# FNet mixing plus gated MLP in split fp32: three instruction moves (y loads, column scaling, second token tile)

## The chip, the cores and the metric

One core of one Trainium2 chip runs the kernel. The metric is the device time of one execution in microseconds. A core has TensorE (PE, with PEld for its weight loads), VectorE (DVE), ScalarE (ACT), GpSimd (POOL) and SyncE (SP), each with an instruction stream of its own that runs in order; SP and POOL also issue DMA transfers, and a DMA issue that must wait holds up all that stands behind it in that stream.

## The reference

With x of 2048 tokens by 640 columns, the function is a sum of three terms over one layer norm:

```
xn  = layernorm(x)
a   = xn @ dft_hid_re.T ; b = xn @ dft_hid_im.T
A   = dft_seq_re @ a - dft_seq_im @ b
g   = xn @ W_gate ; h = (g * (g > 0)) * (xn @ W_up)
out = x + A + h @ W_down
```

All is fp32. W_gate and W_up are 640 x 1728, W_down is 1728 x 640, the sequence matrices are 2048 x 2048.

## The kernel before, in words

Every fp32 product is made of three fp32r matmuls: an operand is split into a high part (ACT copies it rounded, L124) and a low part (DVE subtracts, L125), and `mm3` (L126 to L132) issues high x high, high x low and low x high. On top of that the products use 2x2 block schemes with seven products in place of eight (the names B11, T1, B21, T2, B22, T3, T4).

There are three stages, one after the other on PE.

**Stage 1** (to about 399 us; the layer norm lies in its first 65 us): xn transposed times the sequence matrices. Tokens come in eight groups n = 0 to 7 of 256 tokens, each as two tiles j = 0, 1 of 128 tokens. Groups 0 to 3 lie in the SBUF tile `xs_early`, groups 4 to 7 in `xs_late`; NH = 4. Output columns come in chunks c. At the start the list of work alternates: chunk 0 with group n, then chunk 1 with group n. `first_stream` describes such an entry by a load, a preparation, a run and a finish; `drive(4, 2)` calls the load of an entry, its preparation two entries later, its run four later, its finish five later.

The layer norm of group n+1 is written into the preparation of entry (chunk 1, group n), by `next_group`. Its instructions are pinned: each engine runs them in the order in which they are written. For one group:

- DVE: batch statistics of both tiles (L204, L205), centring of tile 0 (`ln_center`, L225), a reciprocal (listed at L210), centring of tile 1 (L225), four small instructions of a refinement (L218 to L221), the low parts of tiles 0 and 1 (`ln_low`, L235). Groups 0 to 3 norm 384 of the 640 columns this way. The other 256 columns (slice K2, the "lower token columns") are scaled in place by two more instructions at L276, and `keep_a21` (L240) lets POOL issue a DMA that carries them to `xs_early`. Then comes the split of the sequence matrix for (chunk 1, that group), whose low part is L125.
- ACT: the square root (L210), the mean (L213), the high parts of tiles 0 and 1 (`ln_high`, L231), the high part of that split (L124), and the high part of the next chunk-0 matrix (L257).
- POOL: the DMA issue at L240, then one tiny instruction that waits for DVE's split (`behind_vector`, L248), then the two low parts of the next chunk-0 matrix (L255).

PE takes for each group 18 matmuls for chunk 0 (`next_products`, L481: first the six of tile 0 with the high parts of xn, then the six of tile 1, then six with the low parts) and 18 for chunk 1 (L130 to L132). The dictionary `late` carries handles: `late["high"]` and `late["ln"]` are the ACT and DVE instructions after which the chunk-1 split is to be issued.

Groups 0 to 3 of chunk 0 end in three PSUM banks. `keep_first`, called right after the run of group 3, copies them to SBUF on ACT (L121, into `sa`); group 4 then adds to the same banks, so its first three matmuls wait for the three copies.

**Stage 2** (about 399 to 735 us) forms gate and up in 26 rounds (`gate_up`) and a rest (`gate_up_rest`, L927, L928).

**Stage 3** (`project`, to the end) multiplies by the hidden matrices and W_down and adds x, for token half q = 1 and then q = 0. A product such as B11 runs over six units u = 0 to 5. Its entry loads an activation tile `rw` (L1069 from stage 1's results, L1071 from stage 2's) and a weight tile `wr` (L1100), splits both, and runs the matmuls. `get_y` (L1211) loads pieces of x transposed into tiles `y`; three of them belong to B11. It is an entry of its own in the list, placed behind unit 3. `add_y` (L1214) adds the result of a product to `y`. The order of SP and POOL in this stage is the order in which the list is written; DVE and ACT are ordered by the scheduler. The tiles `y` lie where operands of stage 2 lay.

Of the kernel before, what the change touches and what calls it, by code (L numbers as in the profile page):

```python
# [58 lines left out]
def fnet_reglu_kernel(  # L59
# [60 lines left out]
    def copy(o, i):  # L120
        return nc.scalar.activation(o, i, AF.Copy)  # L121
# [108 lines left out]
    def ln_high(g, xs, mv, j, cs):  # L230
        return nc.scalar.activation(ln_parts(g, j, cs)[0], xs[:, j, cs], AF.Copy, scale=mv[:, j, 4:5])  # L231
# [10 lines left out]
    def pin(steps):  # L242
        return [tc.keep_in_program_order(i) for i in steps]
# [6 lines left out]
    def next_group(g, b, raw, before):  # L250

        xs, bs, mv = ln_tiles(g)
        js = slice(0, SG)
        cs = K14 if g < NH else slice(0, D)
        low = lambda engine, j: pin([engine.tensor_tensor(flat(b, 1)[:, j], raw[:, j], flat(b, 0)[:, j].bitcast(F32), op=OP.subtract)])  # L255
        pin(ln_stats(g, xs, bs, mv, js))
        pin([nc.scalar.activation(flat(b, 0), raw, AF.Copy)])  # L257
        if before is not None:
            behind_vector(before)
            for j in range(SG):  # L260
                low(nc.gpsimd, slice(j * CH, (j + 1) * CH))
        root, inverse = ln_first(g, mv, js)
        pin([root])
        pin([ln_mean(g, mv, js)])
        pin([ln_center(xs, mv, 0, cs)])
        pin([inverse()])
        pin([ln_high(g, xs, mv, 0, cs)])
        pin([ln_center(xs, mv, 1, cs)])
        late["high"] = pin([ln_high(g, xs, mv, 1, cs)])[0].ins
        if before is None:  # L270
            for j in range(SG):
                low(nc.vector, slice(j * CH, (j + 1) * CH))
        pin(ln_refine(g, mv, js))
        late["ln"] = pin(ln_low(g, xs, j, cs) for j in range(SG))[-1].ins
        if g < NH:
            late["ln"] = pin(nc.vector.tensor_scalar(xs[:, j, K2], xs[:, j, K2], mv[:, j, 0:1], stat[:, 1, g, j : j + 1],  # L276
                                                     op0=OP.subtract, op1=OP.mult) for j in range(SG))[-1].ins
            keep_a21(g)
        if g == NG - 1:
            nc.sync.dma_start(rows.rearrange("m (g p j) -> p m g j", p=P, j=SG), stat)  # L280
        if g == 2:
            st = stage()[:, :CH].rearrange("p (j d) -> p j d", j=SG)
            for j in range(SG):
                late["high"] = pin([nc.scalar.activation(st[:, j], ln_place(0)[:, j, K2], AF.Copy, scale=stat[:, 1, 0, j : j + 1])])[0].ins
            keep_a21(0, st)

    def first_group(b):

# [244 lines left out]
    def first_stream(c, name, g):  # L533

        t = {}
        half = int(name == "B21")
        n = half * NH + g

        norm = {0: 0 if n == 0 else None, 1: n + 1 if n < NG - 1 else None}.get(c)

        def load():
            if n == 0 and c == 0:
                st = start["raw"] = [raw(), raw()]
                get = lambda c, j: nc.sync.dma_start(st[c][:, j * CH : (j + 1) * CH], dft[c, 0, 0][:, j * CH : (j + 1) * CH])
                ln_load(0, slice(0, 1))
                get(0, 0)
                get(1, 0)
                ln_load(0, slice(1, 2))
                get(0, 1)
                get(1, 1)  # L550
                return
            if norm is not None:
                tc.keep_in_program_order(ln_load(norm, slice(0, SG)))
            if n > 0 or c > 1:
                t["s"] = raw()
                nc.sync.dma_start(t["s"], dft[c, 0, n])
                start[c, n] = t

        def prepare():
            if norm == 0:  # L560
                start["b"] = [(parts(), st) for st in start["raw"]]
                first_group(start["b"])
                return
            if (n > 0 or c > 1) and "b" not in t:
                t["b"] = b = parts()
                with ExitStack() as order:
                    if c == 1:
                        order.enter_context(tc.issue_after(late["ln"]))
                        order.enter_context(tc.issue_after(late["high"]))
                    i = split(flat(b, 0), flat(b, 1), t["s"])  # L570
                if c == 1 and n < NG - 1:
                    late["ln"] = i.ins
            if norm is not None:
                t1 = start[0, norm]
                t1["b"] = parts()
                next_group(norm, t1["b"], t1["s"], flat(b, 1)[:, W2 - 1 : W2] if norm > 1 else None)

        def run():
            if n == 0 and c < 2:
                first_products(c, start["b"])  # L580
                return
            if n > 0 and c == 0:
                next_products(n, t["b"])
                if n == NH - 1:
                    keep_first()
                return
            accs = [(c, ("e1", i)) for i in range(2)]
            with ExitStack() as order:
                if n > 0 and c == 1:
                    order.enter_context(tc.issue_after(start["pe"]))  # L590
                product(g, t["b"], resident(n, 0), accs, half == 0, half == 1, ((c, "v1"), half, half == 0))

        def keep_first():
            t["first"] = sums_a()
            for i, key in enumerate((("e1", 0), ("e1", 1), "v1")):
                pin([copy(t["first"][:, i], E[c, key])])

        def finish():
            if g == NH - 1:
                s = t.get("first")  # L600
                if s is None:
                    s = (sums_a, sums_b)[c % 2]()
                    for i, key in enumerate((("e1", 0), ("e1", 1), "v1")):
                        copy(s[:, i], E[c, key])
                defer(1, lambda: nc.gpsimd.dma_start(pqd[c][0][:, :3] if half else firsts[c], s[:, :3]))

        todo.append((load, prepare, run, finish))
# [451 lines left out]
    def project(q):  # L1059
# [184 lines left out]
        for name in ("B11", "T1", "B21", "T2", "B22", "T3", "T4"):  # L1244
# [4 lines left out]
            for u in range(len(units)):  # L1249
                l, p, r = unit(name, u, u == 0)  # L1250
                end = u == len(units) - 1 and not (tiles and name != "T3")
                todo.append((l, p, r, (lambda name: lambda: read(name))(name) if end else idle))
                if u == 3:
                    todo.append(((lambda name: lambda: get_y(name))(name), idle, idle, idle))
                if name == "B21" and u in (0, 2):
                    (plain_rest if u else plain_block)()
# [50 lines left out]
```

## Time and profile before

| what | value |
|---|---|
| time, median of 3 | 1030.93 us (1029.65 to 1031.65) |
| the profiled execution | 1030.23 us, span 1028.3 us |
| PE busy | 1022.1 us, 4528 matmuls |
| PE weight loads busy | 844.5 us |
| DVE, ACT, POOL busy | 805.9, 427.6, 118.1 us |
| granted PE clock | 1.0 |
| DMA over the span | 236 GB/s |

The time of an execution and the span of its trace differ by 1.93 us, which lie outside the first and last recorded instruction. A timeline row gives the start in us, the length in us, the engine, the line, the operation with the tile written and the tile read, the count of merged instructions, and in brackets the idle time before it with what ended it. A matmul row shows 0.39 us, because matmuls overlap; the distance of two starts, about 0.227 us, is what one costs.

### The profile page before, as it was taken

Reading aid. Unit: us, or ns where it says so; the run is one execution under the profiler, and the core shown is the slowest. Engines: PE = TensorE matmul, PEld = TensorE weight load, DVE = VectorE, ACT = ScalarE, POOL = GpSimd, SP = SyncE. Lnnn points to the kernel's source line nnn. Section 1 sums busy time; section 2 is a strip of 40 time slices with the busy share of each in tenths; the row PEclk is TensorE's granted clock in tenths of the full one; section 3 lists DMA queues with packets and bytes.
Section 4 is the critical chain, followed back from the end, with each engine's and each line's share of the span. In section 5 each row is a group of like instructions: output and inputs, shape, how many; then the busy total and the mean of one; then the engine's idle time right before and its main releaser. Section 6 shows DMA issues by size and latency. Waiting matters only on the chain.

```text
span 1028.3 us, 12486 instructions
## 1 busy us (share of the span) xinstructions
PE 1022.1 (99%) x4528; PEld 844.5 (82%) x4528; DVE 805.9 (78%) x1089; ACT 427.6 (42%) x534; POOL 118.1 (11%) x184
## 2 busy tenths in 40 slices
PE   9999999999999999999999999999999999999998
PEld 7888888888888888888888888888888888888886
DVE  8967987998989586788878988886597666886764
ACT  5554453343433333433335443443355423552531
POOL 3431001012110002411110001000000000000000
PEclk9999999999999999999999999999999999999999
DMA  7987734968969785763474665662699647986543
GB/s 304 342 278 274 265 124 164 338 221 262 349 229 348 299 323 165 249 213 136 153 237 152 225 228 216 230 255 103 237 346 302 189 132 232 357 322 213 156 154 122
DMA packets 101469, 242.73 MB, mean 236 GB/s; under 512 B 11552, under 2 KB 50976, under 8 KB 98848
## 3 DMA queue, kind: packets, MB, share of 16 engines
q1 hardware_dynamic: 83664, 171.68, 48.6%
q0 software_dynamic: 17744, 70.26, 18.6%
q8 instruction: 35, 0.57, 0.2%
q14 instruction: 26, 0.21, 0.1%
HBM read 182.12 MB, written 58.74 MB: 234 GB/s over the span
## 4 chain that ended last, share of the span: by engine, by line
PE 98%; DMA 1%; DVE 0%; SPq 0%; ACT 0%; issue 0%; DVEq 0%
PE ps L132 31%; PE ps L131 31%; PE ps L130 31%; PE ps L481 3%; PE ps L1204 1%; PE ps L510 1%; DMA rw<-hd 1%; DMA r<-in_x 0%; SPq L1211 0%; DVE wt L125 0%; DVE bs L204 0%; DVE y L1214 0%; ACT cb L292 0%; SPq L1100 0%; SPq L1071 0%
## 5 line engine op out<-in xcount | busy, mean ns | idle before, releaser
L132 PE MATMUL ps<-cb,wt 128*128 128x512 f32 x390 | 151.9, 390 | 0.4 <-DVE wt L125 0.4
L130 PE MATMUL ps<-cb,wt 128*128 128x512 f32 x390 | 151.8, 389 | 0.0
L131 PE MATMUL ps<-cb,wt 128*128 128x512 f32 x390 | 151.7, 389 | 0.0
L125 DVE TENSOR_TENSOR cb<-rw,cb 128x1024 fp32r<-128x1024 f32 x83 | 94.0, 1132 | 68.4 <-ACT cb L124 66.9
L124 ACT ACTIVATE cb<-rw 128x1024 fp32r<-128x1024 f32 x83 | 82.0, 988 | 147.3 <-PE ps L132 127.6
L124 ACT ACTIVATE cb<-raw 128x1024 fp32r<-128x1024 f32 x71 | 75.3, 1060 | 114.2 <-PE ps L132 107.8
L125 DVE TENSOR_TENSOR cb<-raw,cb 128x1024 fp32r<-128x1024 f32 x71 | 86.8, 1222 | 40.3 <-ACT cb L124 40.1
L132 PE MATMUL ps<-xs_early,gw 128*128 128x512 f32 x260 | 101.2, 389 | 0.0
L131 PE MATMUL ps<-xs_early,gw 128*128 128x512 f32 x260 | 101.2, 389 | 0.0
L130 PE MATMUL ps<-xs_early,gw 128*128 128x512 f32 x260 | 101.1, 389 | 0.0
L130 PE MATMUL ps<-cb,xs_late 128*128 128x512 f32 x232 | 90.2, 389 | 0.0
L131 PE MATMUL ps<-cb,xs_late 128*128 128x512 f32 x232 | 90.2, 389 | 0.0
L132 PE MATMUL ps<-cb,xs_late 128*128 128x512 f32 x232 | 90.2, 389 | 0.0
L121 ACT ACTIVATE gw<-z 128x1024 fp32r<-128x1024 f32 (+1 forms) x52 | 57.6, 1109 | 76.4 <-DVE z L814 76.4
L131 PE MATMUL ps<-cb,xs_early 128*128 128x512 f32 x226 | 88.0, 390 | 0.0
L132 PE MATMUL ps<-cb,xs_early 128*128 128x512 f32 x226 | 87.9, 389 | 0.0
L130 PE MATMUL ps<-cb,xs_early 128*128 128x512 f32 x226 | 87.9, 389 | 0.0
L132 PEld LDWEIGHTS ps<-cb,wt 128*128 128x128 f32 x390 | 73.2, 188 | 16.0 <-DVE wt L125 0.7
L131 PEld LDWEIGHTS ps<-cb,wt 128*128 128x128 f32 x390 | 73.2, 188 | 15.4
L130 PEld LDWEIGHTS ps<-cb,wt 128*128 128x128 f32 x390 | 73.2, 188 | 15.2
L121 ACT ACTIVATE u<-ps 128x512 f32<-128x512 f32 x52 | 31.1, 597 | 94.0 <-PE ps L132 94.0
L824 DVE TENSOR_TENSOR gw<-z,gw 128x1024 fp32r<-128x1024 f32 (+1 forms) x52 | 64.6, 1283 | 3.8 <-ACT gw L121 3.8
(190 smaller groups left out, 1983.1 us busy)
## 6 DMA issues: line engine op xcount, KB each, us to landing
raw<-in_dft SPq DMA_DIRECT2D x94, 512.0 KB, 5.5
wt<-wparts SPq DMA_DIRECT2D x66, 256.0 KB, 3.2
z<-in_wgu SPq DMA_DIRECT2D x26, 640.0 KB, 4.0
hd<-ob POOLq DMA_DIRECT2D x26, 512.0 KB, 3.7
rw<-hd SPq DMA_DIRECT2D x24, 512.0 KB, 6.4
wparts<-pw POOLq DMA_DIRECT2D x11, 1024.0 KB, 4.1
tk<-in_dft SPq DMA_DIRECT2D x16, 512.0 KB, 6.1
set<-r POOLq DMA_DIRECT2D x16, 512.0 KB, 4.0
```

The source lines that it names most:

```text
L121: return nc.scalar.activation(o, i, AF.Copy)
L124: nc.scalar.activation(hi, src, AF.Copy)
L125: return nc.vector.tensor_tensor(lo, src, hi.bitcast(F32), op=OP.subtract)
L130: nc.tensor.matmul(ps, wh, mh, start=first, stop=False, skip_group_check=more)
L131: nc.tensor.matmul(ps, wh, ml, start=False, stop=False, skip_group_check=more)
L132: nc.tensor.matmul(ps, wl, mh, start=False, stop=last, skip_group_check=more)
L481: start["pe"] = pin([nc.tensor.matmul(E[0, key], xn_part(n * SG + j, d)[v == 1], b[:, int(v == 2), j], start=False, stop=n % NH == NH - 1 ...
L510: pin([nc.tensor.matmul(E[c, key], xn_part(j, d)[v == 1], b[c][0][:, int(v == 2), j], start=j == 0 and v == 0, stop=False)])
L824: tt(self.w[:, 1, cs], self.z[:, cs], self.w[:, 0, cs].bitcast(F32), op=OP.subtract)
L1204: nc.tensor.matmul(B[key], wr[:, v, es], hr[:, cs], start=False, stop=v == 1, skip_group_check=not new)
```

## The change

Three moves of instructions; the matmuls and their order on PE stay as they are, and so does the number of instructions of every kind.

1. `get_y` of B11 for q = 1 goes into the list behind unit 5 in place of unit 3.
2. The two scaling instructions of the lower token columns of groups 1, 2 and 3, with the DMA of `keep_a21`, move out of `next_group` into a function `scale_a21`, which is called right after the split of (chunk 1, that group).
3. For group 4 the high part of tile 1 on ACT and its low part on DVE are issued by `second`, which `keep_first` calls after the three copies.

```diff
@@ next_group
-        late["high"] = pin([ln_high(g, xs, mv, 1, cs)])[0].ins
+        if g != NH:
+            late["high"] = pin([ln_high(g, xs, mv, 1, cs)])[0].ins
...
-        late["ln"] = pin(ln_low(g, xs, j, cs) for j in range(SG))[-1].ins
+        late["ln"] = pin(ln_low(g, xs, j, cs) for j in range(SG)[: 1 if g == NH else SG])[-1].ins
+        if g == NH:
+
+            def second():
+                late["high"] = pin([ln_high(g, xs, mv, 1, cs)])[0].ins
+                late["ln"] = pin([ln_low(g, xs, 1, cs)])[0].ins
+
+            late["second"] = second
         if g < NH:
-            late["ln"] = pin(nc.vector.tensor_scalar(xs[:, j, K2], xs[:, j, K2], mv[:, j, 0:1], stat[:, 1, g, j : j + 1],
-                                                     op0=OP.subtract, op1=OP.mult) for j in range(SG))[-1].ins
-            keep_a21(g)
+            late["a21"] = g, xs, mv
...
+    def scale_a21():
+
+        if "a21" not in late:
+            return
+        g, xs, mv = late.pop("a21")
+        late["ln"] = pin(nc.vector.tensor_scalar(xs[:, j, K2], xs[:, j, K2], mv[:, j, 0:1], stat[:, 1, g, j : j + 1],
+                                                 op0=OP.subtract, op1=OP.mult) for j in range(SG))[-1].ins
+        keep_a21(g)
@@ first_stream, prepare
                 if c == 1 and n < NG - 1:
                     late["ln"] = i.ins
+                    scale_a21()
@@ first_stream, keep_first
                 pin([copy(t["first"][:, i], E[c, key])])
+            late["second"]()
@@ project
-                if u == 3:
+                if u == (len(units) - 1 if (name, q) == ("B11", 1) else 3):
                     todo.append(((lambda name: lambda: get_y(name))(name), idle, idle, idle))
```

## The prediction

> **What bounds the kernel now.** I read the head of the page first, then PE's timeline for every place where two matmul starts lie farther apart than usual, then the waits of PEld, and last the rows of the other engines around those places.
>
> ```profile
> span 1028.3 us, 12486 instructions
> PE 1022.1 (99%) x4528; PEld 844.5 (82%) x4528; DVE 805.9 (78%) x1089; ACT 427.6 (42%) x534; POOL 118.1 (11%) x184
> ```
>
> PE is busy for 99% of the span, and the change leaves it every matmul. So the change can only touch the few holes in PE's stream, or dig new ones. After the start, a matmul begins 0.227 us after the one before it (between the L481 rows at 23.05 and 31.21 lie 36 matmuls, so 8.16/36). These are the places that matter here:
>
> ```profile
> 18.71 0.39 PE L130 MATMUL ps<-cb,xs_early 128*128 128x512 f32 x1
> 19.06 0.50 PE L131 MATMUL ps<-cb,xs_early 128*128 128x512 f32 x1
> 19.40 0.40 PE L132 MATMUL ps<-cb,xs_early 128*128 128x512 f32 x1
> ...
> 23.05 4.24 PE L481 MATMUL ps<-cb,xs_early 128*128 128x512 f32 x18
> ...
> 31.21 4.24 PE L481 MATMUL ps<-cb,xs_early 128*128 128x512 f32 x18
> ...
> 39.37 4.52 PE L481 MATMUL ps<-cb,xs_late 128*128 128x512 f32 x18
> ```
>
> ```profile
> 745.34 0.39 PE L131 MATMUL ps<-cb,wt 128*128 128x512 f32 x1
> 746.08 0.50 PE L132 MATMUL ps<-cb,wt 128*128 128x512 f32 x1 [0.35 <-DVE wt L125]
> 746.42 0.40 PE L130 MATMUL ps<-cb,wt 128*128 128x512 f32 x1
> ```
>
> ```profile
> PEld ps L481 <- ACT sa L121: 0.5, 2, 0.3
> PEld ps L131 <- DVE cb L125: 0.4, 1, 0.4
> ```
>
> Hole 1, at 18.71: distances 0.35 and 0.34 in place of 0.227, so 0.24 us; PEld names DVE's split of chunk 1, group 1. Hole 2, at 39.37: eighteen matmuls of group 4 take 4.52 where those of group 3 take 4.24, so 0.28 us; PEld names the copies into `sa`. Hole 3, at 745.34: distances 0.74 and 0.34, so 0.51 + 0.11 = 0.63 us; PE waited for a weight split of B11's unit 4. After each hole the next matmul is late by about 0.11 too, so I count every stall as its wait plus 0.11. The three holes are 1.15 us together: **no more than that can be won**, 0.11% of the time.
>
> **Move 1, the y loads.** The queue of SP, the consumer of the load, and the first use of `y`:
>
> ```profile
> 726.28 0.48 SPq L1100 DMA_DIRECT2D wr<-in_wd  x1
> 735.10 1.29 SPq L1211 DMA_DIRECT2D y<-in_xt  x3
> 736.44 0.43 SPq L1071 DMA_DIRECT2D rw<-hd  x1
> 736.91 0.47 SPq L1100 DMA_DIRECT2D wr<-in_wd  x1
> ...
> 738.57 1.51 SPq L1069 DMA_DIRECT2D rw<-pq  x1
> ```
>
> ```profile
> SPq L1211 <- PE ps L132: 4.0, 1, 4.0
> ```
>
> ```profile
> 742.84 1.06 ACT L124 ACTIVATE cb<-rw 128x1024 fp32r<-128x1024 f32 x1 [7.16 <-DMA rw<-hd]
> ```
>
> ```profile
> 733.50 0.95 DVE L125 TENSOR_TENSOR wt<-wr,wt 128x768 fp32r<-128x768 f32 x1
> ...
> 755.60 0.68 DVE L1214 TENSOR_TENSOR y<-ps,y 128x512 f32<-128x512 f32 x1
> ```
>
> SP issues nothing from 726.76 to 735.10, because the first y load waits for the last matmul of stage 2, whose memory it takes. Behind it stand the loads of units 4 and 5. ACT gets unit 4's activations at 742.84, that is 6.4 us after their issue at 736.44. With y behind unit 5, the loads of unit 4 and the activations of unit 5 can be issued from 726.8 on. Their tiles are free: `raws` has 24 buffers, and unit 4's weights are the fourth tile of four. Unit 5's weights must wait for the first tile of four to be read, by the DVE row that ends at 734.45. Counting 6.4 to 7.5 us from about 727, unit 4 is there by 734.5, and its split comes right behind unit 3's, some 6 us earlier. Hole 3 goes: **minus 0.63 us**. The y loads themselves still start at 735.1, since the release is PE's, and land some 5 to 7 us later, long before 755.60. What is late next: the loads of T1, issued from 738.57, now follow y directly at about 736.4, so they too are earlier by 2 us. I find no new wait there.
>
> **Move 2, the scaling.** The rows of group 1's tail and group 2's norm on DVE, then POOL:
>
> ```profile
> 17.14 0.73 DVE L276 TENSOR_SCALAR r<-r,mv,stat 128x256 f32<-128x256 f32 x2
> 17.79 1.22 DVE L125 TENSOR_TENSOR cb<-raw,cb 128x1024 fp32r<-128x1024 f32 x1
> 18.93 0.88 DVE L204 BATCH_NORM_STATS2 bs<-r 128x6 f32<-128x320 f32 x2
> ...
> 20.96 1.06 DVE L225 TENSOR_SCALAR r<-r,mv 128x384 f32<-128x384 f32 x1
> ...
> 22.01 0.40 DVE L225 TENSOR_SCALAR r<-r,mv 128x384 f32<-128x384 f32 x1
> ...
> 23.20 1.15 DVE L235 SCALAR_TENSOR_TENSOR xs_early<-r,stat,xs_early 128x384 fp32r<-128x384 f32 x2
> 24.26 0.94 DVE L276 TENSOR_SCALAR r<-r,mv,stat 128x256 f32<-128x256 f32 x2
> ```
>
> ```profile
> 18.20 0.88 POOL L240 DMA_DIRECT2D xs_early<-r  x1 [4.72 <-DVE r L276]
> 19.11 0.20 POOL L248 TENSOR_TENSOR root_t<-cb 128x1 f32<-128x1 f32 x1
> 19.25 2.54 POOL L255 TENSOR_TENSOR cb<-raw,cb 128x512 fp32r<-128x512 f32 x2
> ```
>
> The split moves from 17.79 to 17.14, which fills hole 1: **minus 0.24 us**. Split plus scaling take as long as before, so the statistics still start at 18.93. But the instruction order of the changed kernel keeps POOL's L240 ahead of L248 and L255. Today the DMA issue (0.88, starting 0.33 after the scaling's end) runs beside the split and costs POOL nothing. Behind the change the scaling ends at about 19.0, the issue runs from 19.35 to 20.2, and POOL's two low parts start at 20.4 in place of 19.25: **1.1 us later, for each of groups 1 to 3**. PE does not need those parts for 2 us more. DVE does feel them: the first L225 row takes 1.06 against 0.40 for the second; it starts at 20.96 and ends at 22.02, 0.2 after POOL's pair has ended at 21.79. So centring cannot run while POOL subtracts. What happens when it is due in the first of two subtractions, a later place shows:
>
> ```profile
> 42.88 2.86 POOL L255 TENSOR_TENSOR cb<-raw,cb 128x512 fp32r<-128x512 f32 x2 [0.40 <-ACT cb L257]
> ```
>
> ```profile
> 44.09 0.50 DVE L225 TENSOR_SCALAR r<-r,mv 128x640 f32<-128x640 f32 x1
> ...
> 44.63 1.47 DVE L225 TENSOR_SCALAR r<-r,mv 128x640 f32<-128x640 f32 x1
> ```
>
> The first centring slips in between POOL's two halves (they take 2.86 in place of 2.54), and only the second waits to the end. With POOL 1.1 later, every group from 2 to 4 comes into this case. The Trainium skill, SBUF — State Buffer, section "SBUF: two separate sides", says that the shared ports of VectorE and GpSimd are an exclusive lock, held for one whole instruction; the rows just shown agree, 0.50 for the centring that got in and 1.47 for the one that did not. If the lock were handed on only after POOL's pair, the sum would be that of rival B.
>
> ACT's rows for group 2 give what follows a centring:
>
> ```profile
> 22.13 1.12 ACT L231 ACTIVATE xs_early<-r,mv 128x384 fp32r<-128x384 f32 x2 [0.66 <-DVE mv L210]
> 23.16 0.89 ACT L284 ACTIVATE st<-r,stat 128x256 f32<-128x256 f32 x2
> 23.96 1.04 ACT L124 ACTIVATE cb<-raw 128x1024 fp32r<-128x1024 f32 x1
> ```
>
> Now step by step, as estimates; a high part comes 0.1 behind its centring and takes about 0.6. *Group 2*: the first centring is done at 21.65 + 0.22 = 21.9, about as today. POOL's second half, pushed back by 0.2, ends at 23.1, and the second centring at 23.35 in place of 22.41. The high part of tile 1 is there at 24.0. PE, which starts on the group at 23.05 - 0.24 = 22.81, wants it six matmuls later at 24.2: no stall. The next split waits for ACT: 24.0, then L284 (0.8) and L124 (1.0) give 25.8, and DVE's 1.2 make 27.0. PE wants it as the second matmul of chunk 1, at 22.81 + 19 x 0.227 = 27.1: just in time. *Group 3*: the scaling lies behind that split, so the statistics start at 27.55, and centring is due 2.03 later (18.93 to 20.96), at 29.6. POOL's issue runs from 28.0 to 28.75, its halves from 28.9 to 30.15 and on to 31.6. The first centring is done at 30.4, the high part of tile 0 at about 31.1; PE would be there at 31.21 - 0.24 = 30.97. A stall of about 0.2, with its 0.11: **plus 0.33 us**. *Group 4*, by the same steps: second centring of group 3 at 31.85, split at 33.7, statistics at 35.5, centring due at 37.5 inside POOL's first half (36.8 to 38.1) and done at 38.45, since 640 columns take 0.35 where 384 take 0.22; high part of tile 0, 0.83 long, at 39.4.
>
> **Move 3, the second tile.** ACT's rows today:
>
> ```profile
> 36.79 1.55 ACT L231 ACTIVATE xs_late<-r,mv 128x640 fp32r<-128x640 f32 x2 [0.83 <-DVE mv L210]
> 38.37 1.57 ACT L121 ACTIVATE sa<-ps 128x512 f32<-128x512 f32 x3
> ```
>
> Taken alone, the copies would take the place of the second L231 half, start near 37.55, 0.8 earlier, and end at 39.1, before PE wants them from 39.13 on; tile 1 would be high at 39.95, needed only after six matmuls at 40.5, and its low part on DVE at 41, needed at 42.5. Alone it fills hole 2, minus 0.28. With move 2 ahead of it, tile 0's high part begins at 38.55 in place of 36.79, the copies at 39.3, and they end at 39.9, 40.4 and 40.9. PE, at 39.45, wants them at 39.45, 39.7 and 39.9: it waits for each, in all 1.14 us with the extra 0.11 per wait, where today it loses 0.28: **plus 0.86 us**. The second tile's parts behind the copies (41.6 and 42.5) come just in time, since PE is later as well. From group 5 on there is room: today its second centring ends at 46.1 (the 44.63 row), and PE comes to that tile at 47.8 + 1.36 = 49.2; the high part takes 0.83, which leaves over 2 us, and the shift is 1.7 with PE itself 1 us later.
>
> **The sum.** -0.63 - 0.24 + 0.33 + 0.86 = +0.3 us. On the profiled execution (span 1028.3 and 1.93 around it, 1030.23) that is 1030.5; the profiled run lies 0.7 below the median of the three, inside their spread of 2 us, so against the median of 1030.93 I forecast **1031.2**. The cost of POOL's delay is bounded below by nothing (rival A) and above by both centrings waiting for both halves (rival B).
>
> **The rivals.**
> A, each move does what it is for: if POOL starts its halves less than about 0.5 us later than today, centring ends as today, the chain keeps its lead and all three holes go: -1.15, that is **1029.8**. For it: between groups DVE's work recurs every 7.2 us (17.14, 24.26), PE's every 8.16, so the chain gains 0.95 per group, and 1.1 is only little more. Against it: L240 stands ahead of L255 in POOL's stream and is 0.72 to 0.88 long. 20%.
> B, the slower side: centring gets the ports only when both POOL halves are done, in groups 2 to 4. Each first centring is then some 1.25 later. By the same steps, group 2's tile 0 is high at 23.9 where PE comes at 22.8 (a stall of 1.24), group 3's at 32.75 where PE comes at 32.2 (0.72), and the copies before group 4 cost 1.32. With 0.24 + 0.28 of today's holes taken off, stage 1 is 2.8 us longer; minus 0.63 that is **1033.1**. It decides when centring comes due in the second half, or when the lock is not given at the boundary. Against it stands the 44.09 row; it is one case. 14%.
> C, the y move changes nothing, because the loads of unit 4 wait for something else than y: then 0.63 is not won, **1031.8**. For it: they wait for earlier DMAs of their queue too. Against: SP's wait is put down to PE and y alone. 10%.
>
> **How the numbers follow.** Forecast 52%, A 20%, B 14%, C 10%, and 4% for gains or stalls of other places. A measurement of this kernel can tell about 0.2% (2.06 us) from no change, its runs spread by that much. A and the forecast and C lie within; B lies on the edge, and half of it with some of the rest goes to slower: faster 0.04, same 0.80, slower 0.16. Range 1029.5 to 1033.1: it takes in A and B with some of the runs' spread.
>
> **What would show it.** Step 1: hole at 745 gone, SP's L1071 near 727. Step 2: hole at 18.7 gone; the three L255 pairs from 19.25 on starting about 1.1, 2.2 and 3 us later than today; first L225 short and second long. Step 3: matmuls at 31 late by 0.3, and the first L481 matmuls of `xs_late` spread over more than 4.52. It is wrong if L255 starts at its old times, or if PEld waits for `sa` for less than 0.5 us.

## The result

The changed kernel takes **1033.1 us** (median of 11 runs, 1032.82 to 1035.31) where the kernel before takes 1030.93 (11 runs beside them): a ratio of **1.0025**, 95% interval 1.0018 to 1.0033. The forecast was 1031.2. The span of the profiled execution grew from 1028.3 to 1030.9. The head of the changed kernel's page shows as many matmuls as before. PE's busy time is 1.0 us longer (1023.1 against 1022.1), but a matmul row covers 0.39 us where the next start is due after 0.227, so a short stall counts as busy. The distances of the starts show where the time lies:

```profile
span 1030.9 us, 12484 instructions
...
PE 1023.1 (99%) x4528; PEld 845.3 (82%) x4528; DVE 808.9 (78%) x1089; ACT 426.4 (41%) x534; POOL 118.1 (11%) x184
```

PE's timeline of the changed kernel, at the places that the prediction spoke of (lines of this part of the code are 15 higher than before, those of stage 3 are 17 higher):

```profile
18.75 0.39 PE L130 MATMUL ps<-cb,xs_early 128*128 128x512 f32 x1
18.97 0.39 PE L131 MATMUL ps<-cb,xs_early 128*128 128x512 f32 x1
19.20 0.39 PE L132 MATMUL ps<-cb,xs_early 128*128 128x512 f32 x1
...
22.60 0.39 PE L132 MATMUL ps<-cb,xs_early 128*128 128x512 f32 x1
23.97 4.37 PE L496 MATMUL ps<-cb,xs_early 128*128 128x512 f32 x18 [0.98 <-ACT xs_early L231]
...
32.03 0.39 PE L132 MATMUL ps<-cb,xs_early 128*128 128x512 f32 x1
32.82 4.37 PE L496 MATMUL ps<-cb,xs_early 128*128 128x512 f32 x18 [0.40 <-ACT xs_early L231]
...
40.89 0.39 PE L132 MATMUL ps<-cb,xs_early 128*128 128x512 f32 x1
41.99 3.31 PE L496 MATMUL ps<-cb,xs_late 128*128 128x512 f32 x11 [0.71 <-ACT sa L121]
```

Hole 1 is gone: around 18.97 the starts lie 0.22 to 0.23 apart. In its place three new holes stand, one ahead of each of the groups 2, 3 and 4. Starts that should lie 0.227 apart lie 1.37 and 0.79 apart; with the 0.13 behind each of them (4.37 in place of 4.24 for eighteen matmuls) that is 1.27 and 0.69 us. At group 4 it is 0.87 ahead of the first matmul and 0.64 in the next ones (eleven matmuls take 3.31 where 10 x 0.227 + 0.39 = 2.66 would do), 1.51 us. Together that is 3.47 us; less the 0.24 and 0.28 of holes 1 and 2, stage 1 is 2.95 us longer. These are, within 0.05 for groups 2 and 3 and 0.2 for group 4, the stalls that the prediction gave to **rival B** (1.24, 0.72 and 1.32). What PEld waited for in this stage:

```profile
PEld ps L496 <- ACT xs_early L231: 2.2, 2, 1.4
PEld ps L496 <- ACT sa L121: 1.7, 3, 1.1
```

Those are the high parts of groups 2 and 3 and the copies before group 4. The step before the high parts is the centring. POOL's timeline of the changed kernel:

```profile
19.37 0.88 POOL L240 DMA_DIRECT2D xs_early<-r  x1 [5.86 <-DVE r L298]
20.28 0.20 POOL L248 TENSOR_TENSOR root_t<-cb 128x1 f32<-128x1 f32 x1
20.43 2.54 POOL L255 TENSOR_TENSOR cb<-raw,cb 128x512 fp32r<-128x512 f32 x2
...
29.28 2.54 POOL L255 TENSOR_TENSOR cb<-raw,cb 128x512 fp32r<-128x512 f32 x2
...
37.49 2.52 POOL L255 TENSOR_TENSOR cb<-raw,cb 128x512 fp32r<-128x512 f32 x2
```

and the centrings on DVE's timeline, in the same kernel:

```profile
20.99 2.20 DVE L225 TENSOR_SCALAR r<-r,mv 128x384 f32<-128x384 f32 x1
23.19 0.39 DVE L225 TENSOR_SCALAR r<-r,mv 128x384 f32<-128x384 f32 x1
...
30.03 2.01 DVE L225 TENSOR_SCALAR r<-r,mv 128x384 f32<-128x384 f32 x1
...
38.10 2.28 DVE L225 TENSOR_SCALAR r<-r,mv 128x640 f32<-128x640 f32 x1
```

POOL's pair starts 1.2 us later than before at group 2 (20.43 against 19.25), as forecast. The first centring falls due at 20.99, in the first of the two halves, as forecast too. But it does not come in at that half's end, near 21.7: it takes 2.20 and ends at 23.19, 0.2 behind the *second* half (20.43 + 2.54 = 22.97). The same holds for groups 3 and 4.

In stage 3 hole 3 is gone. SP's queue there:

```profile
729.78 0.47 SPq L1088 DMA_DIRECT2D rw<-hd  x1
...
730.87 0.45 SPq L1088 DMA_DIRECT2D rw<-hd  x1
737.46 0.37 SPq L1117 DMA_DIRECT2D wr<-in_wd  x1
738.04 1.29 SPq L1228 DMA_DIRECT2D y<-in_xt  x3
```

The loads of unit 4 and the activations of unit 5 are now issued by 731.3, unit 5's weights at 737.46, and `y` behind them. Over the whole kernel that is +2.95 - 0.63 = +2.3 us up to the last matmul, and the chain's last addition on DVE starts 2.24 later (1026.31 against 1024.07). The other 0.36 of the span's 2.6 lie behind it, in the last store; I did not follow it.

### The profile page after: what moved, and what is told of

It is laid out like the page before. It is cut to its first block, busy times and chain, and to the rows that moved or that the text cites. A ratio compares the mean times of both kernels' runs of the same rounds, so it can differ in the third digit from the quotient of the medians.

```text
span 1030.9 us, 12484 instructions
## 1 busy us (share of the span) xinstructions
PE 1023.1 (99%) x4528; PEld 845.3 (82%) x4528; DVE 808.9 (78%) x1089; ACT 426.4 (41%) x534; POOL 118.1 (11%) x184
## 4 chain that ended last, share of the span: by engine, by line
PE 95%; DVE 3%; ACT 1%; DMA 0%; issue 0%; DVEq 0%; ACTq 0%
PE ps L132 31%; PE ps L130 31%; PE ps L131 31%; PE ps L496 2%; PE ps L1221 1%; DVE r L225 1%; DVE bs L204 1%; DVE cb L125 0%; DMA r<-in_x 0%; DVE xs_early L235 0%; DVE mv L205 0%; DVE r L298 0%; ACT xs_early L231 0%; DVE cb L255 0%; ACT cb L124 0%
```

## The experiments

Times are medians; each ratio is to the kernel before on the same chip.

**1. The parts.** Moves 1 and 3 with the scaling where it was:

```diff
             late["a21"] = g, xs, mv
+            scale_a21()
...
                     late["ln"] = i.ins
-                    scale_a21()
```

> Moves 1 and 3, with the scaling left ahead of the split as in the kernel before. Lock theory (move 2 puts POOL's DMA issue ahead of its two subtractions, and centring then waits for both): the 3.4 us of stalls at groups 2, 3 and 4 are gone, the holes at 39.4 (0.28) and 745 (0.63) too: about 1030.0, ratio 0.9991. Rival (the stalls come from move 3, the copies pushed ahead of the second tile, or from the y loads): still slower than before, 1032 or more.

Measured: 1029.34, ratio 0.9984 (0.9975 to 0.9994); span 1027.4. Only hole 1 is left.

Move 2 alone (moves 1 and 3 undone):

> Move 2 alone. Lock theory: POOL's L255 pairs start 1.1 us late, the first centring of groups 2 to 4 takes about 2.2 us, stalls of 1.25 and 0.67 at groups 2 and 3, and at group 4 the copies stand behind both high parts, so about 2.4 there, minus hole 1 and hole 2: about +3.8, 1034.7. Rival (move 2 is harmless by itself, minus 0.24): 1030.7.

Measured: 1034.84, ratio 1.0034 (1.0021 to 1.0048). The same first centrings as in the changed kernel (2.20, 2.01, 2.28), the same stalls at groups 2 and 3, and more before group 4 (3.9 us, where 2.4 was expected), where the copies still stand behind the second tile. So the whole loss comes from move 2.

Moves 1 and 3, each alone (its part of the diff of the change, and none of the others):

> The kernel before with the first move alone (the loads of y for B11 behind its last unit). By the sum of the prediction the hole at 745.34 (0.63 us) goes and nothing else changes: 1030.3 in place of 1030.93, ratio 0.9994; last matmul 0.6 us earlier in the profile. By the rival that says the loads didn't hold the split back: ratio 1.0000 and the hole stays.

> The kernel before with the third move alone (second tile of group 4 behind the copies of the sums). By the sum of the prediction the hole at 39.37 (0.28 us) goes and nothing else changes: ratio 0.9997 (1030.65), last matmul 0.3 us earlier in the profile, the weight load's wait for the copies (sa, L121) gone.

Measured: move 1 1029.79, ratio 0.9992 (0.9982 to 1.0002), hole 3 gone; move 3 1030.73, ratio 0.9999 (0.9991 to 1.0008), hole 2 gone. Each time the named hole disappears; neither interval excludes no change. The second one shows why: in that execution hole 3, which move 3 doesn't touch, was larger. PE's timeline of move 3 alone:

```profile
745.73 0.50 PE L130 MATMUL ps<-cb,wt 128*128 128x512 f32 x1 [0.72 <-ACT wt L124]
...
747.13 0.50 PE L132 MATMUL ps<-cb,wt 128*128 128x512 f32 x1 [0.37 <-DVE wt L125]
```

That is 1.9 us in all, against 0.63 in the kernel before. ACT gets unit 4's activations 1.05 us later there than in the kernel before (743.89 against 742.84), and waits for their DMA both times. Hole 3 lay between 0.45 and 2.1 us in the profiled executions that had it.

**2. Is it POOL's delay, or how it comes about?** The theory after the result: something about the DMA issue ahead of POOL's pair keeps the two halves together, so that the centring isn't let in between. The rival: the issue only makes POOL late, and any delay that puts the centring into the first half does the same. A first try put a product of 128x440 (0.92 us, work that nobody reads) ahead of the pair in the kernel before:

```diff
+    fill_t = keep.tile([P, 440], F32, name="fill_t")
...
             behind_vector(before)
+            if g <= NH:
+                pin([nc.gpsimd.tensor_tensor(fill_t, fill_t, fill_t, op=OP.mult)])
             for j in range(SG):
                 low(nc.gpsimd, slice(j * CH, (j + 1) * CH))
```

> The kernel before with one more POOL instruction, a product of 128x440 of about 1.1 us on a tile of its own, ahead of the two subtractions for groups 2 to 4 (its result is used by nobody); DVE and ACT keep their order. Lock theory: the delay of POOL alone does it, first centring 2.1 us long, stalls of about 1.0, 0.3 and 2.4 at groups 2, 3 and 4: about 1034.5. Rival (the order of split and scaling on DVE does it, not POOL): 1030.9, as before.

Measured: 1048.24, ratio 1.0165 (1.0151 to 1.0179), nearly all of it away from the place: matmuls everywhere in stage 1 stood 0.233 us apart. The tile of 1760 bytes a partition had moved every later tile in SBUF. So the run was repeated with 2048 bytes, and once with the 1760 bytes and no product (the first line of the diff, with the tile cleared, and nothing else):

> The kernel before, and for groups 2 to 4 a product of 128x440 on POOL (about 0.92 us, work added, nobody reads it) between POOL's wait (L248) and its two halves, as in the filler run before it, but on a tile of 2048 bytes a partition in place of 1760. If the 1760 bytes alone slowed TensorE there (0.2335 us between matmuls in place of 0.2267), the spacing is 0.2267 again, and what is left is the delay of the halves: first centrings 0.7 to 0.9 us, one wait of about 1.1 us at group 4, ratio 1.001 (1032.0). If the added POOL work itself slowed TensorE, the time stays near 1048 (ratio 1.0165).

> The kernel before with a tile of 1760 bytes a partition set aside in SBUF and cleared once at the start; no other instruction is added, every later tile in SBUF stands at another address. If the addresses slow TensorE: 0.2335 us between matmuls in stage 1 and some 4 ns more each in stage 2, ratio 1.015 (1046.5). If not: ratio 1.000 (1031).

Measured: 1031.77, ratio 1.0019 (1.0011 to 1.0028), with the 2048 bytes; 1046.03, ratio 1.015 (1.0134 to 1.0165), with the layout alone. The layout is nearly the whole of that difference: 15.5 of 16.5 us (more at the end). What the clean run tells of the centring, POOL's and then DVE's timeline:

```profile
19.29 0.20 POOL L250 TENSOR_TENSOR root_t<-cb 128x1 f32<-128x1 f32 x1
19.44 0.92 POOL L263 TENSOR_TENSOR fill_t<-fill_t 128x440 f32<-128x440 f32 x1
20.33 2.66 POOL L257 TENSOR_TENSOR cb<-raw,cb 128x512 fp32r<-128x512 f32 x2
```

```profile
21.14 0.69 DVE L227 TENSOR_SCALAR r<-r,mv 128x384 f32<-128x384 f32 x1
21.83 1.37 DVE L227 TENSOR_SCALAR r<-r,mv 128x384 f32<-128x384 f32 x1
```

POOL is as late as in the changed kernel, the centring falls due in the first half, and here it *does* come in at that half's end (0.69), as the prediction had it. Delay alone doesn't make rival B. The same delay by a DMA issue:

```diff
+    scratch = dram_p.tile([NH + 1, P, SG, D - 3 * P], F32, name="scratch")
...
             behind_vector(before)
+            if g <= NH:
+                pin([nc.gpsimd.dma_start(scratch[g], raw.rearrange("p (j d) -> p j d", j=SG)[:, :, : D - 3 * P])])
             for j in range(SG):
```

> The kernel before, and for groups 2 to 4 one more DMA issue on POOL (of a piece of the input tile to a scratch tensor in DRAM that nobody reads), between POOL's wait for the last subtraction (L248) and its two halves; nothing else is moved. It delays the halves by an issue of about 0.75 to 0.88 us, as the first move does, without touching the scaling, the order on VectorE or the later stages. The three holes of the kernel before stay. Theory D, a DMA issue directly ahead of the two halves lets them run as a pair, so that no centring comes in between: the first centrings of groups 2 to 4 take 1.9 to 2.2 us in place of 0.6 to 0.7, PE waits some 1.1, 0.7 and 1.1 us ahead of them, ratio 1.0025 (1033.5). Theory L, only the delay of the halves counts and the centring that waits comes in at the first half's end: first centrings 0.6 to 0.9 us, one wait of about 1 us at group 4, ratio 1.001 (1032.0).

Measured: 1035.44, ratio 1.0041 (1.0029 to 1.0053), more than either theory gave. In the profiled execution (1036.41) hole 3 was 2.06 in place of 0.63, and PE lost 0.7, 0.35 and 3.9 us at groups 2 to 4, where theory D had 1.1, 0.7 and 1.1. So theory D's waits and time were off; what it had right is the centrings:

```profile
19.52 0.69 POOL L262 DMA_DIRECT2D scratch<-raw  x1
20.14 2.64 POOL L256 TENSOR_TENSOR cb<-raw,cb 128x512 fp32r<-128x512 f32 x2
```

```profile
21.16 1.85 DVE L226 TENSOR_SCALAR r<-r,mv 128x384 f32<-128x384 f32 x1
```

Same place, same delay, a DMA issue in place of a product: the centring waits for both halves.

**3. What opens the pair again.** The changed kernel with a product of one column between the halves, of the first half's last column, so that it must wait for that half:

```diff
-            for j in range(SG):
-                low(nc.gpsimd, slice(j * CH, (j + 1) * CH))
+            low(nc.gpsimd, slice(0, CH))
+            behind_vector(flat(b, 1)[:, CH - 1 : CH])
+            low(nc.gpsimd, slice(CH, W2))
```

> The changed kernel, with a product of one column on POOL between its two halves, which waits for the first half's end (about 0.2 us). Theory H, the two halves run as a pair because the second is already queued when the first ends: with the gap the waiting centring comes in at the first half's end, so the first centrings of groups 2 to 4 take 0.6 to 1.1 us in place of 2.0 to 2.3, only group 4 still waits (0.9 us), ratio 1.0003 (1031.2, what was forecast for the change). Theory N, a centring waits until POOL has no more such work whatever stands between: first centrings 2.2 to 2.5 us, ratio 1.003 (1033.6) or more.

Measured: **1031.11**, ratio 1.0007 (0.9999 to 1.0015). The centring comes in at the first half's end:

```profile
20.50 1.29 POOL L255 TENSOR_TENSOR cb<-raw,cb 128x512 fp32r<-128x512 f32 x1
21.86 0.20 POOL L248 TENSOR_TENSOR root_t<-cb 128x1 f32<-128x1 f32 x1
22.02 1.29 POOL L255 TENSOR_TENSOR cb<-raw,cb 128x512 fp32r<-128x512 f32 x1
```

```profile
21.07 0.94 DVE L225 TENSOR_SCALAR r<-r,mv 128x384 f32<-128x384 f32 x1
```

This is the kernel that the forecast described, and its time is the forecast's (1031.2). PE loses 0.09, 0.28 and 1.36 us there at groups 2, 3 and 4, where the forecast had 0, 0.33 and 1.14, and the profiled span is 0.6 us longer than before (1028.9), where the sum had 0.3. Theory N falls. The same with the column it had already waited for (`behind_vector(before)`), so that nothing waits between the halves:

> The changed kernel, with a product of one column between POOL's two halves, as in the gap run, but of the column that it had already waited for, so that it does not wait for the first half's end. If any instruction between the halves lets the centring in: first centrings 0.8 to 1.1 us, ratio 1.0007 (1031.1, as the gap run). If POOL has to stand still between the halves: first centrings 2.2 to 2.6 us, ratio 1.0025 to 1.003 (1033 to 1034).

Measured: 1033.15, ratio 1.0026 (1.0018 to 1.0035), as the changed kernel. An instruction more is not enough here; a wait is needed.

```profile
20.52 1.29 POOL L255 TENSOR_TENSOR cb<-raw,cb 128x512 fp32r<-128x512 f32 x1
21.78 0.18 POOL L248 TENSOR_TENSOR root_t<-cb 128x1 f32<-128x1 f32 x1
21.93 1.28 POOL L255 TENSOR_TENSOR cb<-raw,cb 128x512 fp32r<-128x512 f32 x1
```

```profile
21.09 2.33 DVE L225 TENSOR_SCALAR r<-r,mv 128x384 f32<-128x384 f32 x1
```

**4. Time since the issue, place, or a wait?** Six column products ahead of the pair in the kernel before; the 128x440 product of the clean run ahead of the pair in the changed kernel; two of them in each kernel:

```diff
             behind_vector(before)
+            for _ in range(6 if g <= NH else 0):
+                behind_vector(before)
             for j in range(SG):
```

```diff
+    fill_t = keep.tile([P, 512], F32, name="fill_t")
...
             behind_vector(before)
+            if g <= NH:
+                for _ in range(2):
+                    pin([nc.gpsimd.tensor_tensor(fill_t[:, :440], fill_t[:, :440], fill_t[:, :440], op=OP.mult)])
             for j in range(SG):
```

> The kernel before, and for groups 2 to 4 six more products of one column on POOL (some 0.15 us each, 0.9 us in all, work added that nobody reads) between POOL's wait (L248) and its two halves. It delays the halves as the filler of 128x440 did, with short instructions and without a DMA issue. Theory D, it is the DMA issue shortly ahead that lets the halves run as a pair: here the centring comes in between them, first centrings 0.7 to 0.9 us, one wait of 1.1 to 1.3 us at group 4, ratio 1.001 (1031.8, as the filler on 2048 bytes). Theory Q, the second half only has to stand ready behind the first, as it does behind any short instructions: first centrings 1.9 to 2.3 us, waits at groups 2, 3 and 4, ratio 1.003 to 1.004 (1034 to 1035).

> The changed kernel, with a product of 128x440 on POOL (0.92 us, work added that nobody reads, on a tile of 2048 bytes) between its wait for the subtraction (L248), which follows the DMA issue, and the two halves of groups 2 to 4. The centring falls due while that product runs. If the effect of the DMA issue is over within the product's time, the centring comes in at the product's end or at the first half's end and takes 0.4 to 1.1 us; the halves then end 1 to 1.5 us later than in the changed kernel, and the second centrings wait for them (1.4 us). If what follows a DMA issue runs through whatever its length, first centrings take about 3.2 us and the time is above 1035.5.

> The kernel before, and for groups 2 to 4 two products of 128x440 on POOL (0.92 us each, work added that nobody reads) between POOL's wait (L248) and its two halves. The centring falls due in the second product, some 1.9 us after POOL's last DMA issue ended. Theory T, a centring is passed over only when a DMA issue ended less than about 1 us before it fell due: it comes in at the second product's end, first centrings 0.3 to 0.7 us. Theory R, a centring that falls due ahead of the pair is passed over until POOL's string ends, DMA issue or not: first centrings 2.7 to 3.1 us. The time is above 1034 by either (the six column products, with the same delay, gave 1036.0); what tells is the centrings.

> The changed kernel, with two products of 128x440 on POOL (0.92 us each, work added that nobody reads) between its wait (L248) and the two halves of groups 2 to 4. The centring falls due in the first product, 0.75 us after the DMA issue ended. If being passed over ends with time (the one product let it wait 2.3 us after the issue's end and no hand-over came), it comes in at the first half's end: first centrings 2.4 to 2.8 us. If it lasts as long as POOL has instructions ready without a gap: first centrings 3.8 to 4.1 us.

Measured: 1036.01, ratio 1.0056 (1.0039 to 1.0073), for the six products. Its time misses both theories' figures, since a column product that waits for the one ahead took 0.26 and not 0.15 us, and POOL was 1.6 us late, not 0.9 (its pair stands 1.78 us behind the start of its wait, 19.61 to 21.39, where it was 0.14). Its centrings (1.44 to 1.61) end 0.2 behind the first half, so theory Q, that any instructions ahead of the pair do it, falls. One product in the changed kernel: 1035.34, ratio 1.0047 (1.0035 to 1.006), centrings of 3.04, 2.88 and 3.17: passed over at two boundaries. Two in the kernel before: 1035.69, ratio 1.0035 (1.0021 to 1.0049), centrings of 0.43, 0.41 and 0.55, at the end of the product in which they fell due: theory R falls. Two in the changed kernel: 1033.35, ratio 1.0028 (1.0017 to 1.0039), centrings of 0.58, 0.40 and 0.70, which neither theory had expected of a DMA issue as near as in the run before it. The difference: the second product there works on the first one's result, and POOL stood still for 0.08 us between them:

```profile
20.36 1.93 POOL L264 TENSOR_TENSOR fill_t<-fill_t 128x440 f32<-128x440 f32 x2
```

```profile
20.93 0.58 DVE L227 TENSOR_SCALAR r<-r,mv 128x384 f32<-128x384 f32 x1
```

Hence theory G and its two runs. Two products on separate columns in the changed kernel; and, with SP issuing the DMA of groups 1 to 3, two products that bring the halves back to where they stand in the changed kernel:

```diff
-                for _ in range(2):
-                    pin([nc.gpsimd.tensor_tensor(fill_t[:, :440], fill_t[:, :440], fill_t[:, :440], op=OP.mult)])
+                for v in (fill_t[:, :256], fill_t[:, 256:]):
+                    pin([nc.gpsimd.tensor_tensor(v, v, v, op=OP.mult)])
```

```diff
-        nc.gpsimd.dma_start(xn_block(g, K2, 0).bitcast(F32), ln_place(g)[:, :, K2] if src is None else src)
+        queue = nc.gpsimd if src is not None else nc.sync
+        queue.dma_start(xn_block(g, K2, 0).bitcast(F32), ln_place(g)[:, :, K2] if src is None else src)
```

> The changed kernel, with two products of 128x256 on POOL (about 0.55 us each, on separate columns, work added that nobody reads) between its wait (L248) and the two halves of groups 2 to 4. The centring falls due in one of the two products, about 0.7 us after the DMA issue ended, with no gap in POOL's string behind it. Theory G, behind a DMA issue the centring comes in only where POOL has a gap: first centrings 3.0 to 3.5 us, 1035.5 to 1036.5. If the gap was not what let it in with the two fillers before: first centrings 0.4 to 1.2 us, 1033 to 1034.

> The changed kernel with the DMA of groups 1 to 3 issued by SP, and two products of 128x440 on POOL (1.9 us in all, work added that nobody reads) between its wait and its two halves, which then start about where they do in the changed kernel, so that the centring falls due some 0.5 to 0.9 us into the first half, with no DMA issue of POOL ahead of it. Theory G, it is the DMA issue that lets the pair run through: here the centring comes in at the first half's end, first centrings 0.7 to 1.1 us, ratio 0.9995 to 1.0005 (1030.2 to 1031.2). If the place alone decides: first centrings 2.0 to 2.3 us, ratio 1.002 (1032.5 to 1033.3).

Measured: 1037.65, ratio 1.0062 (1.0047 to 1.0077), and 1031.99, ratio 1.0011 (1.0002 to 1.0021). In the first of them the centring is passed over at every boundary of the string, three of them at group 2:

```profile
19.45 0.88 POOL L242 DMA_DIRECT2D xs_early<-r  x1 [5.86 <-DVE r L303]
20.35 0.21 POOL L250 TENSOR_TENSOR root_t<-cb 128x1 f32<-128x1 f32 x1
20.50 1.18 POOL L264 TENSOR_TENSOR fill_t<-fill_t 128x256 f32<-128x256 f32 x2
21.65 2.49 POOL L257 TENSOR_TENSOR cb<-raw,cb 128x512 fp32r<-128x512 f32 x2
```

```profile
21.07 3.29 DVE L227 TENSOR_SCALAR r<-r,mv 128x384 f32<-128x384 f32 x1
```

and the second lets it in at the first half's end:

```profile
20.90 2.64 POOL L258 TENSOR_TENSOR cb<-raw,cb 128x512 fp32r<-128x512 f32 x2
```

```profile
21.12 1.29 DVE L227 TENSOR_SCALAR r<-r,mv 128x384 f32<-128x384 f32 x1
```

Both centrings go the way that theory G had it, though not all its sizes hold: the first run is slower than its 1035.5 to 1036.5 (three of its four executions had a granted clock of 0.996 or 0.997; the one at 1.0 took 1036.02), and the second has centrings of 1.29 to 1.42 where 0.7 to 1.1 was expected, and 1031.99 where 1030.2 to 1031.2 was. The second does rule out that the place alone decides, but it can't tell the issue from the wait: its two products are chained, so POOL waits for its own result there too. That it takes the issue is shown by part 2, where a DMA issue and a product stood in the same place. The runs in which the first centrings of groups 2 to 4 fall due while POOL's string still has a boundary ahead (the 1760-byte run, 0.69, 0.73 and 0.89, has its own layout and is left out):

| kernel | on POOL ahead of the boundary | first centrings of groups 2, 3, 4, us | comes in at |
|---|---|---|---|
| changed kernel | issue, then no wait | 2.20, 2.01, 2.28 | string's end |
| move 2 alone | issue, then no wait | 2.20, 2.01, 2.28 | string's end |
| issue by itself | issue, then no wait | 1.85, 2.22, 2.37 | string's end |
| free product between | issue, then no wait | 2.33, 2.13, 2.42 | string's end |
| product behind the issue | issue, then no wait | 3.04, 2.88, 3.17 | string's end |
| two free products | issue, then no wait | 3.29, 3.15, 3.44 | string's end |
| waiting product between | issue, then a wait for POOL's own result | 0.94, 0.78, 1.04 | next boundary |
| two chained products behind the issue | issue, then a wait for POOL's own result | 0.58, 0.40, 0.70 | next boundary |
| product, 2048 bytes | issue, then the wait for DVE's split (see below) | 0.69, 0.74, 0.87 | next boundary |
| two products, before | issue, then the split's wait and one for POOL's own result | 0.43, 0.41, 0.55 | next boundary |
| six column products | issue, then waits | 1.44, 1.47, 1.61 | next boundary |
| two products, issue on SP | no issue; a wait for POOL's own result | 1.29, 1.29, 1.42 | next boundary |

Where POOL issues a DMA and then goes on without a wait, the centring was passed over at every boundary, 18 of 18 times; in the other 18 cases, 15 with a wait behind the issue and three without an issue, it came in at the next one. In two of the 15 (groups 2 and 4 of the product on 2048 bytes) that wait is not visible: the split ends 0.07 and 0.05 us ahead of the issue, and the trace shows POOL standing still in neither. That the wait counts there too is inferred.

**5. The issue out of the way.** All three moves, with the issue behind the pair on POOL:

```diff
-        nc.gpsimd.dma_start(xn_block(g, K2, 0).bitcast(F32), ln_place(g)[:, :, K2] if src is None else src)
+        tc.keep_in_program_order(nc.gpsimd.dma_start(xn_block(g, K2, 0).bitcast(F32), ln_place(g)[:, :, K2] if src is None else src))
...
-        keep_a21(g)
+        late["a21dma"] = g
...
                 low(nc.gpsimd, slice(j * CH, (j + 1) * CH))
+            if "a21dma" in late:
+                keep_a21(late.pop("a21dma"))
```

> All three moves, but POOL issues the DMA of the scaled columns behind its two subtractions. Lock theory: POOL's halves start right behind split and scaling, at about 19.2 as before, the first centring takes about 1.1, and all three holes are filled: about 1029.8, ratio 0.9989. If instead the scaling loses the ports to POOL's halves, which may start once the split is done: its second instruction takes about 2.7 us, statistics come 2.3 us later for each of groups 2 to 4, and the time is 1035 or more. Rival (order on DVE): 1033, as with the change.

and with the issue on SP's queue, as in the last diff of part 4:

> The changed kernel, with the DMA of the scaled columns of groups 1 to 3 issued by SP in place of POOL. POOL's halves then start as soon as the last subtraction is done, about 0.9 us sooner than in the changed kernel. By the prediction's sum without POOL's delay, all three holes gone and nothing in their place: 1029.8, ratio 0.9989; measured with the issue behind the halves, 0.9981 (1029.1). If SP's issue of some 0.6 us holds up a load that PE needs in stage 1, or the scaling itself is late: 1030.9 or more.

Measured: **1029.14**, ratio 0.9981 (0.9973 to 0.999), and **1029.12**, ratio 0.9982 (0.9973 to 0.999). Both beat both kernels. PE's timeline with the issue behind the pair has the three groups at 22.81, 30.97 and 39.13, where the prediction wanted PE if nothing stalls:

```profile
22.81 4.24 PE L498 MATMUL ps<-cb,xs_early 128*128 128x512 f32 x18
...
30.97 4.24 PE L498 MATMUL ps<-cb,xs_early 128*128 128x512 f32 x18
...
39.13 4.24 PE L498 MATMUL ps<-cb,xs_late 128*128 128x512 f32 x18
```

The profiled span is 1.2 us shorter than before (1027.1), the sum of the three holes; the medians differ by 1.8, probably because hole 3 is larger in some executions than in the profiled one (1.9 and 2.06 us in the profiles of two other runs).

## Why the prediction was wrong

**Move 1** was right: hole 3 went, for 0.6 us by the profile and 0.8 in the medians of the run alone. Its working had a wrong step without effect: unit 4's activations were to be split 6 us sooner. ACT's timeline of the changed kernel:

```profile
742.12 1.06 ACT L124 ACTIVATE cb<-rw 128x1024 fp32r<-128x1024 f32 x1 [3.47 <-PE ps L132]
```

ACT waits there for PE to give a buffer back, where it waited for a DMA and started at 742.84 before. PE itself is about 2.95 us later by then, so the split gained some 3.7 us on it; a buffer was late next, and that was enough.

**Move 3** was right alone (hole 2 gone). **Move 2** filled hole 1, and POOL's issue stood ahead of the pair and delayed it by 1.2 us, as worked out.

The step that failed is "The first centring slips in between POOL's two halves [...] With POOL 1.1 later, every group from 2 to 4 comes into this case." It was taken from one place, the centring at 44.09, where POOL had just waited for ACT. In the changed kernel the pair follows a DMA issue without such a wait, and there the centring waits for the whole pair. That costs 1.27 at group 2, 0.69 at group 3 and 1.51 at group 4 in place of 0, 0.33 and 0.86 (with today's 0.28 in the last sum, 1.14): 2.0 us more, the whole miss. The sign that the prediction named for this step, a short first L225 and a long second one, came out the other way round: 2.20 and 0.39 at group 2. With the failed step made true by one waiting column, the time came out at 1031.11. Rival B had the price right to 0.2 us in all (3.28 against 3.47), but its condition ("if the lock is not given at the boundary") had one row against it and was given 14%. The one row differed from the case at hand in what stood ahead of POOL's pair, and the quoted row said so: `[0.40 <-ACT cb L257]`.

Rival A was right on its own condition: where POOL was not delayed, all three holes went and the span was 1.2 us shorter.

Three smaller numbers of the working don't come out of their rows, and none decides anything: from 17.14 to 24.26 is 7.12 and not 7.2, so the chain gains 1.04 a group and not 0.95; 31.1 - 30.97 is 0.13 and not 0.2; and the `y` loads land 2.9 to 4.9 us after their issue in the trace before, not 5 to 7.

Why a wait decides is not visible in these traces, which give one start and one end for POOL as a whole. The Trainium skill has two statements that fit. Its GPSIMD Engine Reference, section "2.1 Instruction dispatch", says that completion of an instruction "does not hold back the next Pool instruction": each of the eight cores behind POOL goes on alone. Its Perfetto Trace Analysis, section "DMA Instruction — SWDGE (GPSIMD)", says that two of the eight write a DMA's descriptors. By these, two cores would be late by the issue (0.7 to 0.9 us here), six would run ahead, and there would be no moment between two halves in which none of the eight reads, until a wait lines them up. The 36 cases of the table don't contradict this; no run here shows single cores, so this stays an explanation. The rule that the prediction used, the exclusive lock in the Trainium skill's SBUF — State Buffer, "SBUF: two separate sides", is not contradicted either: where a centring came in between the halves of the clean run, POOL's pair took 2.66 in place of 2.54. But "held for one whole instruction" is not the time that the other engine waits, 2.2 us here where the first instruction had 0.7 to go.

## What to carry to other kernels

In these runs VectorE's centring was not let in between back-to-back GpSimd instructions if GpSimd had issued a DMA and not waited since. Look for such an issue; putting it behind the work or giving it to another queue brought the kernel to 1029.1 us, and one tiny product that waits for the first half's result to 1031.1. A precedent from the same trace counts only if what stands ahead of it on that engine is the same too, waits included. Where all that a change can win is a tenth of a per cent, price every instruction that it puts ahead of another on a queue first.

## What the runs showed of the hardware

A tile of 1760 bytes a partition, set aside and cleared once, made the matmuls of stages 1 and 2 slower. PE's timeline with the layout alone:

```profile
23.30 4.36 PE L485 MATMUL ps<-cb,xs_early 128*128 128x512 f32 x18
31.70 4.36 PE L485 MATMUL ps<-cb,xs_early 128*128 128x512 f32 x18
```

36 matmuls take 8.40 us in place of 8.16, 0.2333 each, at a granted clock of 0.999; from 450 to 700 us, in stage 2, PE runs 1083 matmuls where it ran 1105, and from 800 to 1000 us, in stage 3, 884 where it ran 882. The time is 1046.03 us in all. A tile of 2048 bytes in the same place left the 1105 of stage 2 as they were. Both are multiples of 16 bytes, the line of SBUF that the Trainium skill names (SBUF — State Buffer, "Specifications (TRN2)"), so that line doesn't tell them apart; 1760 is an odd multiple of 32 bytes. Which tile is hurt by its new address was not tried.
